# Fused attention and two MLP layers on one core: the second layer's weights converted first, layer one after all weights, blocks of one tile

## The chip, the cores and the metric

The kernel runs on one core of one Trainium2 chip. The metric is device time in microseconds (us), from the start to the end of one execution. Before the change it is 1220.09 us, the median of three runs (1217.87 to 1220.64).

## What is computed

The reference is, cut to what matters:

```python
# q, k, v: 4 batches x 8 heads x 576 rows x 64
scores = q @ k.T / 8
kth = 32nd largest of each row of scores
attn = softmax(where(scores >= kth, scores, -1e9))
x = (attn @ v), heads side by side            # 2304 x 512
h = x @ moe_w_in                              # 512 -> 2048
x = maximum(0.01 * h, h) @ moe_w_out          # 2048 -> 512
r = maximum(x @ moe2_w_in, 0)
out = (s * r * r + b) @ moe2_w_out
```

All tensors are float32, and the products are to keep that accuracy.

## The kernel before

Every float32 operand of a matmul is turned into two float16 halves ("hi" and "lo"), and each product is three float16 matmuls: hi x hi, hi x lo, lo x hi. The halves need a power-of-two scale found on the chip, so each of the four weight matrices ("1i", "1o" of layer one, "2i", "2o" of layer two, 16 units of 128 x 512 each) is converted first: `w_load` brings a unit (512 KB) from HBM, `w_rest`, `w_shift`, `w_sign` and `w_round` (ACT, DVE, ACT, POOL) round it to 24 bits, `w_norm` and `w_diag` measure a group of four units on PE and DVE, and `hi`, `lo_g`, `lo_d`, `lo_t` and their kin write the halves. What engine does the splitting is set for each unit by a letter of `WM`. The halves of 1i and 1o stay in SBUF (`wreg`, 32 units). Those of 2i and 2o don't fit: `w_out` stores them to a scratch in DRAM (`sc_2i`, `sc_2o`), and layer two streams them back for every block of rows (`load`, 512 KB for two units, through the four buffers of `wst`); one pair of loads, `kept_i` and `kept_o`, stays (`NRES`).

The 2304 rows are 18 tiles of 128. Attention works in units: one pair of heads of one tile, 72 units, four for a tile. Eight of them, of the two tiles that hold the last 64 rows of two batches each, take twice the matmuls. In a unit, per head: `qk` on PE, `s_ev` on ACT, then on DVE four `t_max` (the eight largest of each row) and three `t_rep` (take them out); the mask and the exponential go by way of DVE (`expo`, `mask`) or by way of POOL and ACT (`above`, `less`, `expo2`), as a letter of `MKE` and `MK` says; the result is split, turned by two DMA transposes (`e_turn`; in the first `EB` units on PE instead) and multiplied with v (`pv_mm`).

When all units of a block's tiles are done, the block goes through layer one and later layer two. `BLOCKS` says how many tiles a block has. `rows_in` scales and splits a tile's rows and turns them by a DMA transpose (`turn`). In `layer`, `m_in` multiplies one unit of the first weight (12 matmuls of 128 x T, T being 128 times the tiles of the block) into `h`, `a1` to `a5` apply the activation and split it (ACT and POOL), and `m_out` multiplies into `acc` (3 matmuls of 128 x 512 for a unit and a tile). A token `lane` lets one layer at a time run its `m_in`. Layer one's `a1` waits for `fin1`, the scales of 1i and 1o; layer two waits for `fin`, everything converted and stored.

The order of the work is set by a planner: `Plan.add` notes each step with its engine, an assumed duration, its dependences and a key, and `Plan.order` lets each engine take, whenever it is free, the ready step with the lowest key whose buffers are there. The result is a fixed order on every engine. All the numbers in the tables at the top (`W0`, `WD`, `KO`, `PAD`) are keys or allowances of this planner. Before the change, the keys place 1i and 1o first, 2o and 2i later among the attention units.

Of the kernel before, what the change touches and what calls it, by code (L numbers as in the profile page):

```python
# [13 lines left out]
I32 = mybir.dt.int32  # L14
# [51 lines left out]
PAD = {"e_turn": 0, "load": 0.65, "turn": 0, "PE": 0}  # L66
# [137 lines left out]
def kernel(  # L204
# [44 lines left out]
    PHASED = ("wst", "raw", "T", "nred", "cI", "hl")  # L249
# [4 lines left out]
              "wT": (flat_w, 512 * NU + 4096)}  # L254
# [106 lines left out]
    out_done, lo_done, scaled, rounded = {}, {}, {}, {}  # L361
    g_last, cs_last, gtok = None, None, None
    for m, f in order:
# [4 lines left out]
        def w_load(m=m, f=f):  # L368
            t = ring("wraw" if m == "1i" else "raw", [P, 1024], I32, f"raw_{m}_{f}")
            raw[m, f] = t  # L370
            w = wsrc[m].bitcast(I32)
            if m[1] == "i":
                nc.sync.dma_start(out=t.rearrange("p (c n) -> p c n", c=4),
                                  in_=w[:, 2 * P * f:2 * P * (f + 1)].rearrange("(c p) n -> p c n", p=P))
            else:
                nc.sync.dma_start(out=t, in_=w[P * f:P * (f + 1), :])

        def w_rest(m=m, f=f):

            wT[m, f] = ring("wT" if m == "1i" else "T", [P, 512], F32, f"T_{m}_{f}")  # L380
# [245 lines left out]
    for (b, p), U in sorted(first_unit.items(), key=lambda e: e[1]):  # L626
# [65 lines left out]
        def v_hi(b=b, p=p, i=i):  # L692
            vt = vhl[b, p] = vbufs[i % BUFS["vT"]]
            r = vn[b, p]
            nc.scalar.activation(r[:, 0:9, :], r[:, 0:9, :], AF.Copy, scale=cv[b, p])
            nc.scalar.copy(vt[:, 0, 0:512].rearrange("p (h r d) -> p h r d", h=2, r=4),
                           r.rearrange("p (h r) d -> p h r d", h=2)[:, :, 0:4, :])
            for h in range(2):
                a, c = slice(64 * h, 64 * h + 64), slice(512 + 64 * h, 576 + 64 * h)
                nc.scalar.copy(vt[a, 0, c], r[a, 4, :])  # L700

        def v_lo(b=b, p=p):
            vt, r = vhl[b, p], vn[b, p]
            nc.gpsimd.tensor_tensor(vt[:, 1, 0:512].rearrange("p (h r d) -> p h r d", h=2, r=4),
                                    r.rearrange("p (h r) d -> p h r d", h=2)[:, :, 0:4, :],
                                    vt[:, 0, 0:512].rearrange("p (h r d) -> p h r d", h=2, r=4), op=ALU.subtract)
            for h in range(2):
                a, c = slice(64 * h, 64 * h + 64), slice(512 + 64 * h, 576 + 64 * h)
                nc.gpsimd.tensor_tensor(vt[a, 1, c], r[a, 4, :], vt[a, 0, c], op=ALU.subtract)
# [18 lines left out]
    for u in range(NUN):  # L728
# [170 lines left out]
        for c, (j0, j1) in enumerate(((0, 4), (4, 8), (8, 9)) if u < EB else ()):  # L899
# [384 lines left out]
```

## Time and profile before

| | |
|---|---|
| median of three runs | 1220.09 us |
| the profiled execution, its time and its span | 1219.95 us, 1218.1 us |
| instructions in the span | 24846 |
| PE busy | 1054.8 us, 87% |
| DVE busy | 927.3 us, 76% |
| ACT busy | 888.8 us, 73% |
| POOL busy | 808.9 us, 66% |
| granted TensorE clock, mean | 0.94 |
| mean busy share of the 16 DMA engines (dynamic queue) | 66.3% |

PE is TensorE's matmuls, PEld its weight loads, DVE is VectorE, ACT ScalarE, POOL GpSimd, SP the engine that issues all DMAs. A matmul's busy time is modelled from a pipelined engine, so how fast PE goes is better read from the distance between the starts of two groups of a timeline. The granted clock is a share of full speed: 1.00 is 2.4 GHz, 0.50 would be 1.2 GHz.

### The profile page before, as it was taken

The numbers are of one execution on the slowest core, as the hardware profiler recorded it, in microseconds if no ns is written. First come the engines' busy times: TensorE is split into PE (matmuls) and PEld (weight loads), VectorE is DVE, ScalarE is ACT, GpSimd is POOL, SyncE is SP. The second block draws the span as 40 slices with busy tenths as digits, with TensorE's granted clock in tenths as the row PEclk, the third lists the DMA queues.
The fourth block names the chain that finished last, engine by engine and source line by source line (L and its number), as shares of the span: only waits on it lengthen the run. The fifth ranks groups of instructions, "written<-read, shape, count | busy, mean of one in ns | idle before, by whom it ended". The sixth has DMA issues, their size and how long they took to land.

```text
span 1218.1 us, 24846 instructions
## 1 busy us (share of the span) xinstructions
PE 1054.8 (87%) x8952; PEld 720.7 (59%) x8952; DVE 927.3 (76%) x2189; ACT 888.8 (73%) x1679; POOL 808.9 (66%) x1138
## 2 busy tenths in 40 slices
PE   2556665459979997999899999999999999999998
PEld 1324433236556755776666677676567776766665
DVE  3689899889995999998879999974996599710100
ACT  6999885587678777878888887876887486742432
POOL 6876444567667786868888787885886477832321
PEclk9676888679989998999999999999999999999999
DMA  8936355486878756984579986445797578662454
GB/s 260 295 56 186 121 182 188 131 203 150 210 131 217 188 105 118 233 164 85 106 147 223 245 210 147 76 93 139 178 225 202 99 155 214 128 175 78 137 190 141
DMA packets 349244, 198.84 MB, mean 163 GB/s; under 512 B 277696, under 2 KB 302272, under 8 KB 349120
## 3 DMA queue, kind: packets, MB, share of 16 engines
q1 hardware_dynamic: 349120, 197.25, 66.3%
q8 instruction: 70, 1.15, 0.4%
q14 instruction: 54, 0.44, 0.1%
HBM read 122.16 MB, written 13.11 MB: 111 GB/s over the span
## 4 chain that ended last, share of the span: by engine, by line
PE 37%; DVE 23%; ACT 15%; POOL 9%; DMA 8%; issue 5%; SPq 2%; DVEq 0%; ACTq 0%; POOLq 0%
PE h L1098 14%; PE acc L1168 14%; DVE mx L829 9%; DVE wk L838 8%; PE pv L973 3%; PE sc L811 2%; DMA a<-ehl 2%; POOL ehl L939 2%; ACT em L870 2%; POOL em L867 2%; POOL g L1146 1%; DMA raw_2i<-in_moe_w_in_dram 1%; ACT ehh L933 1%; DVE em L854 1%; DMA st_o<-sc_2o 1%
## 5 line engine op out<-in xcount | busy, mean ns | idle before, releaser
L829 DVE MAX8 mx<-wk 128x8 f32<-128x576 f32 x432 | 312.4, 746 | 0.7
L1168 PEld LDWEIGHTS <-g 128*128 128x128 f16 x1728 | 164.1, 99 | 141.0 <-issue 12.9
L1098 PE MATMUL h<-early,wreg 128*128 128x256 f16 (+1 forms) x1920 | 215.1, 263 | 0.5 <-ACT r L1127 0.5
L1168 PE MATMUL acc<-wreg,g 128*128 128x512 f16 x864 | 215.2, 379 | 0.0
L838 DVE MATCH_REPLACE8 wk<-mx,wk 128x576 f32<-128x576 f32 x288 | 212.7, 741 | 0.0
L1098 PEld LDWEIGHTS <-wreg 128*128 128x128 f16 x1920 | 174.8, 98 | 50.3 <-issue 1.1
L1168 PE MATMUL acc<-st_o,g 128*128 128x512 f16 x756 | 190.3, 379 | 1.7 <-DMA st_o<-sc_2o 1.7
L1098 PE MATMUL h<-xT,st_i 128*128 128x256 f16 (+1 forms) x1680 | 187.5, 262 | 0.4 <-ACT r L1130 0.2
L939 POOL TENSOR_TENSOR ehl<-em,ehh 128x576 f16<-128x576 f32 x130 | 167.3, 1293 | 16.4 <-DMA a<-ehl 7.5
L1098 PEld LDWEIGHTS <-st_i 128*128 128x128 f16 x1680 | 151.9, 98 | 42.4 <-DMA st_i<-sc_2i 1.4
L867 POOL TENSOR_TENSOR em<-s,em 128x576 f32<-128x576 f32 x96 | 136.0, 1431 | 19.2 <-ACT em L864 19.0
L1146 POOL TENSOR_TENSOR g<-early,g 128x512 f16<-128x512 f32 x72 | 83.4, 1159 | 72.2 <-ACT g L1143 71.8
L811 PE MATMUL sc<-kT,qT 128*128 128x288 f16 (+1 forms) x640 | 104.1, 303 | 29.9 <-ACT s L817 24.3
L1143 ACT ACTIVATE g<-r 128x512 f16<-128x512 f32 x144 | 89.7, 624 | 50.4 <-PE acc L1168 49.9
L1146 POOL TENSOR_TENSOR g<-r,g 128x512 f16<-128x512 f32 x72 | 84.7, 1177 | 62.1 <-ACT g L1143 60.1
L829 DVE MAX8 mx<-s 128x8 f32<-128x576 f32 x144 | 107.8, 749 | 12.6 <-ACT s L817 12.4
L817 ACT COPY s<-sc 128x576 f32<-128x576 f32 x144 | 91.2, 633 | 24.6 <-PE sc L811 24.1
L838 DVE MATCH_REPLACE8 wk<-mx,s 128x576 f32<-128x576 f32 x144 | 106.7, 741 | 0.0
L864 ACT ACTIVATE em<-s,st 128x576 f32<-128x576 f32 x96 | 71.1, 769 | 39.4 <-POOL st L858 35.4
L811 PEld LDWEIGHTS <-qT 128*128 128x128 f16 (+1 forms) x640 | 59.5, 106 | 63.4 <-issue 44.9
L933 ACT CAST ehh<-em 128x576 f16<-128x576 f32 x130 | 86.6, 667 | 13.4 <-DVE em L854 12.2
L870 ACT ACTIVATE em<-em,st,est 128x576 f32<-128x576 f32 x96 | 82.8, 863 | 15.0 <-POOL em L867 14.5
(209 smaller groups left out, 1745.5 us busy)
## 6 DMA issues: line engine op xcount, KB each, us to landing
st_i<-sc_2i SPq DMA_DIRECT2D x70, 512.0 KB, 4.3
st_o<-sc_2o SPq DMA_DIRECT2D x70, 512.0 KB, 4.3
raw_1o<-in_moe_w_out_dram SPq DMA_DIRECT2D x16, 512.0 KB, 4.2
wreg<-in_moe_w_in_dram SPq DMA_DIRECT2D x16, 512.0 KB, 6.3
raw_2o<-in_moe_w_out_dram SPq DMA_DIRECT2D x16, 512.0 KB, 3.4
raw_2i<-in_moe_w_in_dram SPq DMA_DIRECT2D x16, 512.0 KB, 4.4
qn<-in_q_dram SPq DMA_DIRECT2D x16, 256.0 KB, 4.2
sc_2o<-hl_2o SPq DMA_DIRECT2D x16, 256.0 KB, 2.7
```

Of the source, the lines that this page charges most:

```text
L811: nc.tensor.matmul(pt[a, c, 0:288], lhsT=qT[u][:, h, z, a], rhs=kT[b, p][:, 576 * h + 288 * c:576 * h + 288 * c + 288], start=(z == 0), st ...
L817: nc.scalar.copy(sc[u, h], box["pt"][:, :, 0:288])
L829: nc.vector.max(out=mx[u][:, h, r, :], in_=wk[u, h] if r else flat(sc[u, h]))
L838: nc.vector.match_replace(out=wk[u, h], in_to_replace=mx[u][:, h, r, :], in_values=src, imm_value=NEG)
L867: nc.gpsimd.tensor_tensor(em[u][:, h, :], flat(sc[u, h]), em[u][:, h, :], op=ALU.subtract)
L870: nc.scalar.activation(em[u][:, h, :], em[u][:, h, :], AF.Exp, bias=st[u][:, h:h + 1], scale=est[:, 0, u:u + 1], accum_out=st[u][:, 2 + h: ...
L933: nc.scalar.copy(ehl[u][0][:, 576 * h:576 * h + 576], em[u][:, h, :])
L939: nc.gpsimd.tensor_tensor(ehl[u][1][:, a], em[u][:, h, :], ehl[u][0][:, a], op=ALU.subtract)
L1098: nc.tensor.matmul(box["h"][:, n * T:(n + 1) * T], lhsT=w[:, ew, c, :], rhs=src[:, ex, c, :], start=(c == 0 and ew == 0 and ex == 0), stop ...
L1143: nc.scalar.activation(gt[:, 0], box["r1"], AF.Square if l else AF.Copy)
L1146: nc.gpsimd.tensor_tensor(ghl[i, l, g][:, 1], box["v"], ghl[i, l, g][:, 0], op=ALU.subtract)
L1168: nc.tensor.matmul(accs[i, l, tt], lhsT=ghl[i, l, g][:, eg, n * T + tt * P:n * T + (tt + 1) * P], rhs=w[:, ew], start=(f == 0 and eg == 0 ...
```

## The change

The order of the weights becomes 2o, 2i, 1i, 1o. Since `wreg` is empty until 1i and 1o are converted, its upper half (1o's place) serves 2o, 2i and 1i as landing and work buffers (`wraw`, four, and `wT`, eight), and eight units of its lower half serve as buffers for the halves of 2o and 2i on their way to DRAM (`hl`, eight in place of two). Units 8 to 15 of 1i therefore wait until units 8 to 15 of 2i have been stored. 1o lands in `raw` and `T` (eight in place of six). Layer one can start only when 1i and 1o, now the last, are done. The 18 tiles form 16 blocks of one tile and one of two, in place of eight blocks of two and two of one. The planner's keys, the splitting modes `WM`, the mask modes `MKE`, and `PAD` get other values; `SQ`, which names the engine of the squaring, is "A" in both. New options for keys and values (`KVM`, all "G") choose what was done before; one of `EBM`'s letters is "D", which moves three small subtractions of unit 2 from PE and ACT to DVE (`e_low`).

```diff
-... "raw": 2, "T": 6, "hl": 2, "wraw": 4, "wT": 8, "wst": 4,
+... "raw": 2, "T": 8, "hl": 8, "wraw": 4, "wT": 8, "wst": 4,
-WM = {"1i": "GAPP", "1o": "PPDP", "2o": "VPAV", "2i": "APPG"}
-ORDER = ("1i", "1o", "2o", "2i")
+WM = {"1i": "PDAA", "1o": "DAAG", "2o": "GPPV", "2i": "PPAV"}
+ORDER = ("2o", "2i", "1i", "1o")
-MKE = "DDDDDDDDADDADDADDAADAADA"
+MKE = "DADADADAAAAADADAAADADADA"
-EB = 7
+EB = 6
-W0 = {"1i": -32.95, "1o": -81.15, "2o": 9.16, "2i": -16.52}
-WD = {"1i": 0.038, "1o": 0.182, "2o": 0.322, "2i": 1.5}
+W0 = {"2o": -38.54, "2i": -51.71, "1i": -9.33, "1o": 3.35}
+WD = {"2o": 0.024, "2i": 0.068, "1i": 0.375, "1o": 0.199}
-KO = {"wl": -16.16, "wh": -41.37, "k": -33.06, "v": -8.31, "q": -56.3, "u0": 5.64, "u1": 11.13, "u2": -2.91, "kt": -33.14, "qh": -19.39}
+KO = {"wl": 15.86, "wh": 13.91, "k": -28.68, "v": -34.52, "q": -44.01, "u0": -4.83, "u1": 2.14, "u2": 32.26, "kt": -16.55, "qh": -21.94}
-BLOCKS = [2, 2, 2, 2, 2, 2, 1, 1, 2, 2]
+BLOCKS = [1, 1, 1, 1, 1, 1, 1, 1, 1, 1, 1, 1, 1, 1, 1, 1, 2]
-PAD = {"e_turn": 0, "load": 0.65, "turn": 0, "PE": 0}
+PAD = {"e_turn": 0, "load": 0, "turn": 4.29, "PE": 0}
...
-              "wT": (flat_w, 512 * NU + 4096)}
+              "wT": (flat_w, 512 * NU + 4096), "hl": (flat_w, 8 * 512)}
...
-            t = ring("wraw" if m == "1i" else "raw", [P, 1024], I32, f"raw_{m}_{f}")
+            t = ring("raw" if m == "1o" else "wraw", [P, 1024], I32, f"raw_{m}_{f}")
-            wT[m, f] = ring("wT" if m == "1i" else "T", [P, 512], F32, f"T_{m}_{f}")
+            wT[m, f] = ring("T" if m == "1o" else "wT", [P, 512], F32, f"T_{m}_{f}")
...
-            free = None if m != "1o" else lo_done["1i", ff] if ff >= 8 else rounded["1i", 12 + ff // 2]
+            if m == "1o":
+                free = [lo_done["1i", ff] if ff >= 8 else rounded["1i", 12 + ff // 2]]
+            else:
+                free = [x_ for x_ in (out_done[order[16 + ff]], cs_done.get(order[16 + ff]))] if m == "1i" and ff >= 8 else []
...

```

How it moves the order, at two places. First DVE, where the scales of layer one are finished. `w_shift` is L387 before, `t_max` and `t_rep` are L860 and L869 after, `lo_d` is L498 before, the last row of `fin1` is L585 before and L594 after. Before:

```order
L387 SCALAR_TENSOR_TENSOR T_2o_1264<-raw_2o_1190,T_2o_1264 128x512
L453 TENSOR_SCALAR cI_1o_1286<-ident,cg 128x128
L576 TENSOR_REDUCE consts<-cg 128x1
L325 TENSOR_SCALAR cg<-cg 128x4
L578 TENSOR_SCALAR cg<-cg,consts 128x4
L580 TENSOR_SCALAR consts<-consts 128x1
L576 TENSOR_REDUCE consts<-cg 128x1
L325 TENSOR_SCALAR cg<-cg 128x4
L578 TENSOR_SCALAR cg<-cg,consts 128x4
L580 TENSOR_SCALAR consts<-consts 128x1
L585 SCALAR_TENSOR_TENSOR cg<-cg 128x4
L498 SCALAR_TENSOR_TENSOR wreg<-T_1o_1117,cg,wreg 128x512
```

After:

```order
L860 MAX mx_2388<-s_1_2347 128x8
L860 MAX mx_2388<-wk_0_2392 128x8
L869 MATCH_REPLACE wk_1_2402<-mx_2388,s_1_2347 128x576
L585 TENSOR_REDUCE consts<-cg 128x1
L328 TENSOR_SCALAR cg<-cg 128x4
L587 TENSOR_SCALAR cg<-cg,consts 128x4
L589 TENSOR_SCALAR consts<-consts 128x1
L585 TENSOR_REDUCE consts<-cg 128x1
L328 TENSOR_SCALAR cg<-cg 128x4
L587 TENSOR_SCALAR cg<-cg,consts 128x4
L589 TENSOR_SCALAR consts<-consts 128x1
L594 SCALAR_TENSOR_TENSOR cg<-cg 128x4
```

Before, `fin1` stands at DVE's instruction 197, with 2o and 2i still to come; now it stands at 382, among the searches of unit 10 (`mx_2388` is that unit's buffer), with the rounding of all 64 units of weights ahead of it.

Second SP, where the first weights of layer two are fetched back. L943 and L980 are `e_turn` (the number behind `a_` is the attention unit), L1044 and L1081 `turn`, L781 and L812 `q_turn`, L1192 and L1229 the kept pair, L1077 and L1114 `load`. Before:

```order
L540 DMA sc_2i<-hl_2i_3042 128x1024
L1044 DMA_TRANSPOSE early<-xhl_2_3050 128x8x128
L943 DMA_TRANSPOSE a_13_3201<-ehh_3122 128x9x128
L781 DMA_TRANSPOSE qT_3218<-qhl_2965 128x8x128
L1192 DMA kept_i_3241<-sc_2i 128x2x1024
L1192 DMA kept_o_3247<-sc_2o 128x2x1024
L943 DMA_TRANSPOSE a_13_3261<-ehl_3162 128x9x128
L1077 DMA st_i_3271<-sc_2i 128x2x1024
L1077 DMA st_i_3276<-sc_2i 128x2x1024
L1077 DMA st_i_3284<-sc_2i 128x2x1024
L1077 DMA st_o_3291<-sc_2o 128x2x1024
L739 DMA qn_3298<-in_q_dram 128x8x64
```

After:

```order
L980 DMA_TRANSPOSE a_8_2386<-ehl_2372 128x9x128
L1081 DMA_TRANSPOSE early<-xhl_1_2296 128x8x128
L980 DMA_TRANSPOSE a_9_2555<-ehh_2513 128x9x128
L980 DMA_TRANSPOSE a_9_2584<-ehl_2535 128x9x128
L812 DMA_TRANSPOSE qT_2620<-qhl_2237 128x8x128
L1229 DMA kept_i_2660<-sc_2i 128x2x1024
L1229 DMA kept_o_2665<-sc_2o 128x2x1024
L1114 DMA st_i_2674<-sc_2i 128x2x1024
L1114 DMA st_i_2705<-sc_2i 128x2x1024
L1114 DMA st_i_2710<-sc_2i 128x2x1024
L1114 DMA st_i_2720<-sc_2i 128x2x1024
L770 DMA qn_2774<-in_q_dram 128x8x64
```

The kept pair and the first loads stood between the two transposes of unit 13 and right behind; they now stand ahead of those of unit 10, and behind them follow 238 loads in all, 14 for each of 17 blocks, where there were 140 for ten blocks.

## Rows read from the trace of the kernel before

**Rows 1.** The page, parts 1 and 2: engines, and the span in 40 slices.

```profile
span 1218.1 us, 24846 instructions
PE 1054.8 (87%) x8952; PEld 720.7 (59%) x8952; DVE 927.3 (76%) x2189; ACT 888.8 (73%) x1679; POOL 808.9 (66%) x1138
...
PE   2556665459979997999899999999999999999998
...
DVE  3689899889995999998879999974996599710100
...
PEclk9676888679989998999999999999999999999999
DMA  8936355486878756984579986445797578662454
```

**Rows 2.** Windows: stretch, length, busy us per engine, granted clock, DMA share, GB/s.

```profile
0.00:273.00 273.00, 150.69 (x862) 89.00 (x862) 220.38 (x517) 217.97 (x419) 167.08 (x230) 0.77 0.63 180
273.00:348.00 75.00, 64.51 (x543) 43.14 (x541) 73.02 (x178) 53.74 (x100) 53.48 (x70) 0.93 0.72 169
348.00:480.00 132.00, 120.81 (x1112) 86.28 (x1113) 111.96 (x277) 101.85 (x195) 96.04 (x153) 0.96 0.69 154
480.00:1080.00 600.00, 584.47 (x5538) 413.75 (x5536) 510.26 (x1198) 469.68 (x893) 457.88 (x659) 1.00 0.72 161
1080.00:1218.00 138.00, 134.32 (x907) 88.56 (x905) 11.64 (x23) 45.56 (x76) 34.44 (x30) 1.00 0.46 144
```

**Rows 3.** Timeline of PE where layer one starts: start, us, line, tiles, idle before.

```profile
271.99 1.57 PE L973 MATMUL pv<-vhl,a 128*128 128x128 f16 x25 [3.65 <-DMA a<-ehl]
273.37 3.99 PE L1098 MATMUL h<-early,wreg 128*128 128x256 f16 x24
```

**Rows 4.** Timeline of PE at two later waits.

```profile
347.94 4.25 PE L1098 MATMUL h<-xT,kept_i 128*128 128x256 f16 x24 [2.14 <-DMA xT<-xhl]
...
460.87 1.12 PE L811 MATMUL sc<-kT,qT 128*128 128x288 f16 x4 [5.77 <-ACT s L817]
```

**Rows 5.** Timeline of PE in a one-tile block, 936 to 939, and 1000 to 1009.

```profile
936.20 0.83 PE L1098 MATMUL h<-early,wreg 128*128 128x128 f16 x12
936.87 0.65 PE L811 MATMUL sc<-kT,qT 128*128 128x288 f16 x4
937.36 0.81 PE L1168 MATMUL acc<-st_o,g 128*128 128x512 f16 x3
938.01 0.83 PE L1098 MATMUL h<-early,wreg 128*128 128x128 f16 x12
...
1000.46 2.17 PE L1098 MATMUL h<-xT,st_i 128*128 128x128 f16 x36
1002.47 0.65 PE L811 MATMUL sc<-kT,qT 128*128 128x288 f16 x4
...
1004.36 1.47 PE L1098 MATMUL h<-early,wreg 128*128 128x256 f16 x12
1005.67 1.03 PE L973 MATMUL pv<-vhl,a 128*128 128x128 f16 x27
1006.53 1.47 PE L1098 MATMUL h<-early,wreg 128*128 128x256 f16 x12
```

**Rows 6.** The page, part 5: groups' count, busy us, mean ns.

```profile
L829 DVE MAX8 mx<-wk 128x8 f32<-128x576 f32 x432 | 312.4, 746 | 0.7
L838 DVE MATCH_REPLACE8 wk<-mx,wk 128x576 f32<-128x576 f32 x288 | 212.7, 741 | 0.0
L867 POOL TENSOR_TENSOR em<-s,em 128x576 f32<-128x576 f32 x96 | 136.0, 1431 | 19.2 <-ACT em L864 19.0
L1098 PEld LDWEIGHTS <-wreg 128*128 128x128 f16 x1920 | 174.8, 98 | 50.3 <-issue 1.1
```

**Rows 7.** Groups by line on DVE and POOL: the mask, rounding, splitting.

```profile
L854 DVE SCALAR_TENSOR_TENSOR em<-s,mx,em 128x576 f32<-128x576 f32 x48 | 45.7, 956 | 5.8 <-ACT em L851 5.5
L387 DVE SCALAR_TENSOR_TENSOR wreg<-wreg 128x512 int32<-128x512 int32 x16 | 16.1, 1016 | 9.1 <-ACT wreg L382 9.0
L387 DVE SCALAR_TENSOR_TENSOR T_2o<-raw_2o,T_2o 128x512 int32<-128x512 int32 x16 | 11.6, 722 | 1.2 <-ACT T_2o L382 1.2
```

**Rows 8.** Waits of SP's queue: line, releaser, us in total, times, longest.

```profile
SPq L376 <- POOL T_1o L397: 26.8, 8, 11.7
SPq L376 <- POOL T_2o L397: 26.5, 11, 8.0
```

**Rows 9.** DMA issues by line (count, KB, us to landing), and one window of 80 us.

```profile
st_i<-sc_2i SPq DMA_DIRECT2D x70, 512.0 KB, 4.3
st_o<-sc_2o SPq DMA_DIRECT2D x70, 512.0 KB, 4.3
...
640.00:720.00 80.00, 78.12 (x689) 54.93 (x689) 78.59 (x185) 68.25 (x131) 65.75 (x99) 1.00 0.96 228
```

**Rows 10.** Waits of PE for streamed weights, in all.

```profile
PE acc L1168 <- DMA st_o<-sc_2o: 1.7, 2, 1.1
```

More of the change, by code (lines that the diff above doesn't have):

```diff
@@ L420 @@
         x = add(ACT, REST, w_rest, [l], kk, take=[tT], use=[tr])
-        y = add(DVE, 0.62, w_shift, [x], kk, use=[tT, tr], lock=True)
+        y = add(DVE, 0.66, w_shift, [x], kk, use=[tT, tr], lock=True)
         x = add(ACT, SIGN, w_sign, [x], kk, use=[tr])
@@ L528 @@
                 x = add(PE, 0.86, lo_t, [i_], ks, take=[th] + out_tok, use=tI + [tT])
-                x = add(ACT, 0.478, hi_p, [x, free], ks, use=[th] + out_tok)
+                x = add(ACT, 0.478, hi_p, [x, *free], ks, use=[th] + out_tok)
                 if mode == "V":
@@ L669 @@
         ick_done[b, p] = add(DVE, 0.07, k_inv, [x], kk)
-        x = add(ACT, 0.667, k_scale, [x], kk, use=[tk])
-        x = add(ACT, 0.573, k_hi, [x], kk, use=[tk, th])
-        x = add(POOL, 1.234, k_lo, [x], kk, use=[tk, th])
+        if KVM[i] == "D":
+            x = add(ACT, 0.667, k_hi, [x], kk, use=[tk, th])
+            x = add(DVE, 0.75, k_low, [x], kk, use=[tk, th], lock=True)
+        else:
+            x = add(ACT, 0.667, k_scale, [x], kk, use=[tk])
+            x = add(ACT, 0.573, k_hi, [x], kk, use=[tk, th])
+            x = add(POOL, 1.234, k_lo, [x], kk, use=[tk, th])
         tok_kT[b, p] = token("kT")
@@ L698, in v_hi @@
             for h in range(2):
                 a, c = slice(64 * h, 64 * h + 64), slice(512 + 64 * h, 576 + 64 * h)
[L700 to L709, printed above, removed]
+                out.append((lambda e, a=a, c=c: vt[a, e, c], r[a, 4, :], a))
@@ L717 @@
         x = chain(DVE, pow2_steps(lambda b=b, p=p: cv[b, p], lambda box=box: box["pt"][:, 0:1], 1, 0.13), [x], key + KO["v"] + 0.2, use=[tt])
-        x = add(ACT, 1.63, v_hi, [x], key + KO["v"] + 0.2, use=[tv], take=[tV])
-        vT_done[b, p] = add(POOL, 1.65, v_lo, [x], key + KO["v"] + 0.2, use=[tv, tV])
+        x = add(ACT, 1.0 if KVM[i] == "D" else 1.63, v_hi, [x], key + KO["v"] + 0.2, use=[tv], take=[tV])
+        if KVM[i] == "D":
+            vT_done[b, p] = add(DVE, 1.0, v_lo, [x], key + KO["v"] + 0.2, use=[tv, tV], lock=True)
+        else:
+            vT_done[b, p] = add(POOL, 1.65, v_lo, [x], key + KO["v"] + 0.2, use=[tv, tV])
     qn, qhl, qT, icq_done, sc, wk, em, mx, st, ehl, ahl, pv, x32 = {}, {}, {}, {}, {}, {}, {}, {}, {}, {}, {}, {}, {}
@@ L926 @@
             x = add(ACT, 0.05 + 0.107 * n, e_hi2, [x, lo[0][0] if c else None], ke, use=[tt, *ta])
-            y = add(PE, 0.15 + 0.053 * n, e_sub, [x], ke, use=[tt, *ta])
-            lo.append((x, add(ACT, 0.05 + 0.107 * n, e_lo2, [y], ke, use=[tt, *ta])))
+            if EBM[u] == "D":
+                lo.append((x, add(DVE, 0.1 + 0.13 * n, e_low, [x], ke, use=[tt, *ta])))
+            else:
+                y = add(PE, 0.15 + 0.053 * n, e_sub, [x], ke, use=[tt, *ta])
+                lo.append((x, add(ACT, 0.05 + 0.107 * n, e_lo2, [y], ke, use=[tt, *ta])))
         def e_hi(u=u, h=0):
```

58 lines of the change are left out of this document (42 added, 16 removed).

## The prediction

> **What bounds the kernel now.** I read the engines and the slices first [rows 1]. PE is busy for 87% of the span, at 90% or more from the 17th slice on, while DVE is done at slice 35 of 40. The first quarter is different: PE is half idle and its granted clock mostly 0.6 to 0.9, DVE and ACT are busy. So there is a first stage in which PE waits for others, and a second in which PE is the bound. The windows put numbers on it [rows 2]: to 273 us PE has 151 us of work; from 480 to 1080 it is idle for 15.5 of 600 us, in the last 138 us for 3.7, which are the last output's way out. Layer one starts at 273.37 us [rows 3].
>
> So the time is: start of layer one, plus PE's work from there, plus what PE loses on the way. I price PE's work by distances between starts, not by busy times [rows 5]. Twelve matmuls of 128 x 256 take 1.31 us (1004.36 to 1005.67), twelve of 128 x 128 take 0.67 us (936.20 to 936.87), three of 128 x 512 take 0.65 us (937.36 to 938.01), four of `qk` 0.49 us (936.87 to 937.36), 27 of `pv_mm` 0.86 us (1005.67 to 1006.53). A tile in one layer has 16 units: 16 x (0.655 + 0.65) = 20.88 us in a block of two, 16 x (0.67 + 0.65) = 21.12 us alone. A unit of attention is 2 x 0.49 + 0.86 = 1.84 us, the eight double ones twice that.
>
> Before, from 273 us: 32 tile-layers in pairs and 4 alone are 752.7 us; attention has by PE's order 59 `qk` units and 62 `pv` units left, with the double ones 67 x 0.98 + 70 x 0.86 = 126 us; the rest of 2i is about 6 us (an estimate from its few matmuls). Sum 885 us. PE ends at about 1214 us, so 56 us are lost. Of these I find 21.7 us idle from 273 to 480 us, 9 us by the clock there (0.93 and 0.96), 15.5 us idle later [rows 2]; some 10 us remain in small gaps.
>
> **The change, part by part.** All sums are made against the profiled execution: span 1218.1 us, 1.85 us more around it, 1219.95 us, which is the median of the runs within 0.1 us.
>
> *Order of the weights.* No step is added; all 64 units are converted ahead of layer one rather than 60 or so. What counts is the work that stands ahead of it on each engine, and attention gets less: nine `pv` units done at layer one's start in place of ten. On DVE, up to the scales of layer one, against DVE's work up to 273 us before: 4 searches and 3 replacements fewer (7 x 0.75 = 5 us less), 10 masks fewer (9.6 us less), 6 roundings more (4.3 to 6.1 us more), some 5 us more of small splits [rows 6, 7]. Sum: about 4 us less. ACT comes out about 4 us longer by the same count. POOL has 11 more splits, 3 more roundings and 10 more of `less`, about 26 us, on top of the 167 it was busy for in 273 us. POOL is the least loaded of the three in that stretch, DVE and ACT stand idle for some 55 us each [rows 2], so I cost POOL's part at nothing; if it lay wholly on the path it would be 26 us. Against it, loads of weights waited 53 us in all for their two landing buffers [rows 8], and now have four. Some of the idle time should close. I take layer one's start at 272 us; the ends are 258 (a quarter of the idle time closes) and 299 (POOL's 26 us in full).
>
> *Blocks of one tile.* Seven blocks of two are split: 7 x 2 layers x 16 units x (2 x 0.67 - 1.31 = 0.03 us) = 6.7 us more on PE. The weight loads double with the small matmuls, and one takes 98 ns on PEld [rows 6], longer than the 56 ns between two such matmuls, but rows of 36 in sequence still run at 2.01/36 = 56 ns [rows 5], so they hide. Here a rule speaks against the change: the Trainium skill ("TensorE: Matmul & The Clock Gate", section "Back-to-back issue gap") gives about 81 ns for each matmul in a sustained stream with 128 columns. By that the split would cost (81 - 56) ns for each of 5376 new matmuls, an estimate of 134 us; this trace has 56 ns, so I keep 6.7 us.
>
> PE's work from 272 us is then 32 x 21.12 + 4 x 20.88 = 759.4 us, less 2.7 us for 48 matmuls that PE does early; attention has 60.5 `qk` and 63 `pv` units left, 128 us; no weights. Sum 885 us, the same as before.
>
> *What PE loses early.* Before, 31 us to 480 us. The waits there are layer two's first matmuls waiting for the block's turned rows, and PE held in order behind a `qk` whose score buffer is not free [rows 4]. Layer one has a pair of tiles then, and the next pair needs eight more units of attention. With single tiles, two whole tiles are ready when layer one starts, and each next one needs four units. By PE's order, 15 `pv` units (double ones counted twice) stand ahead of 42 us of layer work before and of about 68 us after; at 31 units it is 160 and 198 us. I take 10 us.
>
> *Loads of layer two.* 17 blocks x 14 loads are 238 in place of 140. In the last window the DMA engines move 144 GB/s at a share of 0.46, 313 GB/s when busy, so 512 KB take 1.67 us; 98 more take 164 us of all 16 engines. From 273 us on the engines are busy for 0.72 x 75 + 0.69 x 132 + 0.72 x 600 + 0.46 x 138 = 641 us [rows 2]; it becomes 805 us. By PE's order 125 us of layer work remain behind the last `pv_mm` (141 before); it takes some 40 loads, 67 us. So 738 us of transfers fall between 272 us and the end of attention, where PE has 760 us of work and perhaps 805 us to do it in: a share of 0.92. Before, it was about 0.72, with 0.96 for one stretch of 80 us, in which PE still lost only 1.9 us [rows 9]. Waits for streamed weights were 1.7 us [rows 10]. That cover, transfers with room to spare, is what the change uses up. I add one wait of about 0.6 us for each block, 10 us, to the late loss of 23.
>
> SP issues 98 more DMAs, and a `load` that waits for its `wst` buffer holds the `e_turn` and `turn` behind it, which release `pv_mm` and `m_in`; I cost that within the same 10 us, since attention is ahead: DVE's searches end over 100 us before PE does.
>
> Sum: 272 + 885 + 10 + 33 = 1200, plus 3.8 to the end of the span and 1.85 around it: **1206 us**, 14 less than before.
>
> **The rivals.**
> *The DMA engines become the bound (slower).* For: a share of 0.92 for 800 us, four buffers, 4.3 us from issue to landing [rows 9], one queue in order. Against: 0.96 was sustained for 80 us. The end of attention is then 272 + 738/share, and 125 + 6 us follow. At 0.90 it is 1223 us; that is the point from which it decides. At 0.87 it is 1251 us.
> *The start moves further.* If a quarter of the idle time closes: 258 + 885 + 38 + 6 = 1187 us. For: waits for buffers [rows 8]. Against: POOL's 26 us.
> *Nothing is gained.* What the early stage wins is lost later: 273 + 885 + 56 + 6 = 1220 us. So too if the single blocks only shift the waits that single pairs had.
> *Small matmuls wait for their weight loads.* 98 ns each rather than 56: 5376 x 42 ns = 226 us more, 1430 us. Only the rule above speaks for it, and by its own figure it would be less; rows 5 speak against.
>
> **How the numbers follow.** Forecast 0.42, start earlier 0.12, nothing gained 0.12, DMA bound 0.32, small matmuls 0.02. A measurement of this kernel tells 0.2%, 2.4 us, from no change. Of "nothing gained" I put 0.08 within that and 0.02 on each side, so: faster 0.56, same 0.08, slower 0.36. The forecast's own range is 1195 to 1217 us, from the start's ends and the late loss. The range over the cases goes from 1182 (an early start with somewhat fewer losses) to 1252 (DMA at 0.87).
>
> **What would show it.** Right: layer one's twelves come at 0.67 us distance and start near 272 us; from there PE is idle for under 45 us; the DMA share is about 0.9 to the end of attention; the tail behind the last `pv_mm` is near 125 us. Wrong: waits of PE or PEld for `st_i` and `st_o` of tens of us, or `pv_mm` waiting for `a` again and again (DMA bound); a start after 290 us (POOL on the path); twelves at 1 us (weight loads).

## The result and the profile after

The changed kernel takes **1208.3 us**, the median of six runs (1204.23 to 1211.08); the kernel before takes 1220.37 us beside it (six runs). The ratio is 0.9903, with a 95% interval of 0.9884 to 0.9923: faster by about 12 us. The forecast was 1206 us, 14 us less than before. The profiled execution took 1208.34 us, 1206.6 us of it the span.

The page, parts 1 and 2, answers to [rows 1]:

```profile
span 1206.6 us, 30307 instructions
PE 1044.3 (87%) x11589; PEld 754.8 (63%) x11589; DVE 918.5 (76%) x2164; ACT 892.5 (74%) x1696; POOL 844.5 (70%) x1169
...
PE   1675666239999999999999989999999999999988
...
PEclk9876677658999999999999999999999999999999
DMA  8987872347799999989999998999898998974274
```

PE's row jumps from 3 to 9 at the 10th slice and stays there but for a few 8s, where it dipped to 7 twice before. The price is in the last row: the DMA engines, mostly at 4 to 8 before, are at 9 in 20 of the 40 slices. The windows, with the columns of [rows 2]:

```profile
0.00:273.00 273.00, 143.50 (x884) 90.29 (x885) 222.25 (x491) 222.66 (x430) 203.77 (x250) 0.73 0.68 195
273.00:348.00 75.00, 73.35 (x925) 56.25 (x923) 73.04 (x180) 57.98 (x111) 55.17 (x78) 0.97 0.83 171
348.00:480.00 132.00, 127.97 (x1603) 94.72 (x1603) 101.78 (x256) 101.53 (x196) 95.62 (x149) 1.00 1.00 234
480.00:1080.00 600.00, 583.39 (x7311) 436.58 (x7307) 516.37 (x1222) 470.49 (x897) 461.24 (x669) 1.00 0.96 224
1080.00:1207.00 127.00, 116.07 (x876) 76.94 (x876) 5.11 (x19) 39.84 (x66) 28.73 (x25) 0.98 0.49 156
```

From 273 to 480 us PE is idle for 1.7 + 4.0 = 5.7 us, where it was idle for 21.7; from 480 to 1080 us for 16.6 (15.5 before); behind that for 10.9 of 127 us (3.7 before). The timeline of PE, with the columns of [rows 3], at the start of layer one, at the longest later wait, at the last `pv_mm` and in the tail. (Four units of layer one's `m_in`, 48 matmuls, run ahead of it, from 194.44 us on; what follows them has to wait for the scales of 1i and 1o.)

```profile
272.19 4.00 PE L1135 MATMUL h<-early,wreg 128*128 128x128 f16 x36 [2.76 <-ACT r L1164]
...
278.33 0.83 PE L1135 MATMUL h<-early,wreg 128*128 128x128 f16 x12
279.00 0.81 PE L1205 MATMUL acc<-wreg,g 128*128 128x512 f16 x3
...
713.73 2.00 PE L1135 MATMUL h<-xT,st_i 128*128 128x128 f16 x24 [4.14 <-DMA st_i<-sc_2i]
...
1067.62 1.03 PE L1010 MATMUL pv<-vhl,a 128*128 128x128 f16 x27
...
1150.04 1.46 PE L1205 MATMUL acc<-st_o,g 128*128 128x512 f16 x6 [2.08 <-DMA st_o<-sc_2o]
1153.95 1.41 PE L1205 MATMUL acc<-st_o,g 128*128 128x512 f16 x5 [2.46 <-DMA st_o<-sc_2o]
...
1195.81 6.85 PE L1205 MATMUL acc<-st_o,g 128*128 128x512 f16 x31
```

PE's waits for transfers in the whole span (us, times, longest):

```profile
PE acc L1205 <- DMA st_o<-sc_2o: 11.8, 12, 2.5
PE pv L1010 <- DMA a<-ehl: 10.8, 7, 4.3
PE h L1135 <- DMA st_i<-sc_2i: 9.0, 9, 4.1
```

The first and third make 20.8 us of waits for streamed weights, some 19 more than before [rows 10]. In exchange, other waits between 480 and 1080 us are gone. This is that stretch in the kernel before, for the score buffer and for the scaled rows:

```profile
PE sc L811 <- ACT s L817: 6.1, 7, 2.4
PE acc L1168 <- ACT xs L1020: 4.3, 4, 2.1
```

In the changed kernel the first is 0.8 us there, and the second no longer appears. The DMA issues, answering to [rows 9], take 0.6 to 0.8 us longer to land:

```profile
st_i<-sc_2i SPq DMA_DIRECT2D x119, 512.0 KB, 4.9
st_o<-sc_2o SPq DMA_DIRECT2D x119, 512.0 KB, 5.1
```

### The profile page after: what moved, and what is told of

Same layout as the page of the kernel before. It is cut to its first block, busy times and chain, and to the rows that moved or that the text cites. A ratio compares the mean times of both kernels' runs of the same rounds, so it can differ in the third digit from the quotient of the medians.

```text
span 1206.6 us, 30307 instructions
## 1 busy us (share of the span) xinstructions
PE 1044.3 (87%) x11589; PEld 754.8 (63%) x11589; DVE 918.5 (76%) x2164; ACT 892.5 (74%) x1696; POOL 844.5 (70%) x1169
## 4 chain that ended last, share of the span: by engine, by line
PE 43%; DVE 17%; DMA 12%; ACT 11%; POOL 11%; issue 4%; SPq 2%; DVEq 0%; POOLq 0%; ACTq 0%
PE h L1135 17%; PE acc L1205 17%; DVE mx L860 7%; DVE wk L869 6%; DMA st_o<-sc_2o 4%; PE pv L1010 3%; PE sc L842 3%; POOL ehl L976 2%; DMA a<-ehl 2%; POOL g L1183 2%; DMA st_i<-sc_2i 2%; POOL em L898 2%; ACT wreg L386 1%; ACT wreg L397 1%; ACT em L901 1%
## 5 line engine op out<-in xcount | busy, mean ns | idle before, releaser
L860 DVE MAX8 mx<-wk 128x8 f32<-128x576 f32 x432 | 313.2, 747 | 0.9
L1135 PEld LDWEIGHTS <-wreg 128*128 128x128 f16 x3264 | 211.0, 99 | 54.0 <-issue 6.4
L1135 PE MATMUL h<-early,wreg 128*128 128x128 f16 (+1 forms) x3264 | 235.1, 224 | 2.8 <-ACT r L1164 2.8
L1205 PE MATMUL acc<-wreg,g 128*128 128x512 f16 x864 | 231.3, 379 | 0.0
L869 DVE MATCH_REPLACE8 wk<-mx,wk 128x576 f32<-128x576 f32 x288 | 212.8, 741 | 0.0
L1205 PE MATMUL acc<-st_o,g 128*128 128x512 f16 x756 | 200.6, 382 | 12.5 <-DMA st_o<-sc_2o 11.8
L1135 PEld LDWEIGHTS <-st_i 128*128 128x128 f16 x2856 | 179.7, 98 | 48.9 <-DMA st_i<-sc_2i 12.5
L1135 PE MATMUL h<-xT,st_i 128*128 128x128 f16 (+1 forms) x2856 | 201.4, 223 | 9.1 <-DMA st_i<-sc_2i 9.0
L898 POOL TENSOR_TENSOR em<-s,em 128x576 f32<-128x576 f32 x110 | 155.9, 1432 | 22.9 <-ACT em L895 22.7
L860 DVE MAX8 mx<-s 128x8 f32<-128x576 f32 x144 | 107.9, 750 | 23.0 <-ACT s L848 22.7
L895 ACT ACTIVATE em<-s,st 128x576 f32<-128x576 f32 x110 | 82.2, 768 | 41.9 <-POOL st L889 37.5
L901 ACT ACTIVATE em<-em,st,est 128x576 f32<-128x576 f32 x110 | 94.7, 862 | 17.1 <-POOL em L898 16.8
L869 DVE MATCH_REPLACE8 wk<-mx,s 128x576 f32<-128x576 f32 x144 | 106.8, 742 | 0.0
L1180 ACT ACTIVATE g<-r 128x512 f16<-128x512 f32 x144 | 89.5, 622 | 18.5 <-PE acc L1205 17.8
L1167 ACT ACTIVATE r<-h,cg 128x512 f32<-128x512 f32 x72 | 49.1, 682 | 67.0 <-PE h L1135 65.9
```

The lines of the kernel that those rows point to most:

```text
L860: nc.vector.max(out=mx[u][:, h, r, :], in_=wk[u, h] if r else flat(sc[u, h]))
L869: nc.vector.match_replace(out=wk[u, h], in_to_replace=mx[u][:, h, r, :], in_values=src, imm_value=NEG)
L895: nc.scalar.activation(em[u][:, h, :], flat(sc[u, h]), AF.Relu, bias=st[u][:, 8 + h:9 + h], scale=-BIG)
L898: nc.gpsimd.tensor_tensor(em[u][:, h, :], flat(sc[u, h]), em[u][:, h, :], op=ALU.subtract)
L901: nc.scalar.activation(em[u][:, h, :], em[u][:, h, :], AF.Exp, bias=st[u][:, h:h + 1], scale=est[:, 0, u:u + 1], accum_out=st[u][:, 2 + h: ...
L1135: nc.tensor.matmul(box["h"][:, n * T:(n + 1) * T], lhsT=w[:, ew, c, :], rhs=src[:, ex, c, :], start=(c == 0 and ew == 0 and ex == 0), stop ...
```

## The experiments

The question is which part of the change holds the 12 us: the order of the weights, the blocks of one tile, or the numbers that the planner got with them; and what the loads cost. Ratios are against the kernel before, run beside each set.

**1. The order of the weights alone.** In the changed kernel:

```diff
-BLOCKS = [1, 1, 1, 1, 1, 1, 1, 1, 1, 1, 1, 1, 1, 1, 1, 1, 2]
+BLOCKS = [2, 2, 2, 2, 2, 2, 1, 1, 2, 2]
```

> The changed kernel with the blocks of before (eight of two tiles, two of one) and all else of the change: the order of the weights alone. The planner plans anew. Theory (the blocks of one tile won the early stage and paid for it in loads): PE is idle again for 18 to 25 us between the start of layer one and 480 us (5.7 us in the changed kernel), the waits for st_i and st_o fall from 20.8 us to under 4, the twelves of 128 columns become 256 (6.7 us less), the tail's waits for st_o go; sum 1208 + 23 - 18 - 6.7 + about 5 for waits of pairs on their rows = 1212, between 1207 and 1220. Rival A (the order of the weights won the early stage, the single blocks only cost): the early idle time stays under 10 us and 20 to 25 us of waits and small matmuls go, 1183 to 1192. Rival B (order and blocks are worth something only together): 1220 or more, with layer one starting later than 280 us because a pair needs eight units.

Measured: 1249.6 us, ratio 1.0251 (1.0234 to 1.0267), slower than either kernel. Windows and timeline of PE:

```profile
273.00:348.00 75.00, 56.81 (x473) 39.64 (x473) 69.59 (x178) 48.42 (x93) 48.20 (x66) 0.89 0.58 122
348.00:480.00 132.00, 120.78 (x1107) 83.80 (x1105) 106.14 (x255) 101.89 (x196) 96.12 (x156) 0.94 0.69 152
480.00:1080.00 600.00, 562.49 (x5258) 396.35 (x5255) 518.36 (x1215) 461.42 (x875) 455.12 (x661) 0.98 0.69 157
```

```profile
326.33 1.12 PE L842 MATMUL sc<-kT,qT 128*128 128x288 f16 x4 [4.51 <-ACT s L848]
...
337.80 1.18 PE L842 MATMUL sc<-kT,qT 128*64 128x288 f16 x8 [6.02 <-ACT s L848]
```

The early idle time came back, as the theory had it, and more of it (18.2 + 11.2 = 29.4 us up to 480, where the theory said 18 to 25). But 37.5 us of idle time between 480 and 1080 us came too, and no theory had that. The start is at 274.74 us, so that rival B's reason, a later start, isn't it. Three times, at 321, 446 and 569 us, PE has no layer matmul for 15 to 21 us: a pair is through and the next one isn't ready.

**2. The blocks alone.** In the kernel before:

```diff
-BLOCKS = [2, 2, 2, 2, 2, 2, 1, 1, 2, 2]
+BLOCKS = [1, 1, 1, 1, 1, 1, 1, 1, 1, 1, 1, 1, 1, 1, 1, 1, 2]
```

> The kernel before with sixteen blocks of one tile and one of two, and nothing else of the change: the blocks alone, in the old order of the weights. Theory: the early idle time falls from 21.7 us to about 8, 98 loads more bring waits of some 20 us for st_i and st_o, small matmuls 6.7 us: between 1203 and 1215, about 1208, and the start of layer one near 273 us. Rival A (the order of the weights is what counts): early idle time over 18 us, and the loads' cost on top, 1230 to 1245. Rival B (only both together): layer one starts earlier than 265 us, since one tile needs four units, but layer two's first weights come later than one tile's layer one, so that PE waits over 20 us for them before 400 us; 1215 to 1230.

Measured: 1237.73 us, ratio 1.0167 (1.0139 to 1.0194).

```profile
273.00:348.00 75.00, 59.62 (x720) 43.70 (x719) 73.86 (x185) 53.88 (x98) 48.81 (x80) 0.95 0.83 205
348.00:480.00 132.00, 121.89 (x1516) 89.94 (x1516) 102.23 (x253) 96.53 (x186) 91.58 (x142) 0.99 0.92 219
```

PE is idle for 25.5 us from 273 to 480 us. The number is rival A's, but the first experiment spoke against rival A. The start is rival B's: layer one begins at 157 us and does one tile by 198 us. Then it has no matmul for 72 us, until the second tile's turned rows are there (rival B had PE wait for layer two's weights):

```profile
270.26 1.44 PE L1098 MATMUL h<-early,wreg 128*128 128x128 f16 x12 [1.18 <-DMA early<-xhl]
```

Each part alone loses, so either both belong together, or the planner's keys, which the change sets anew, fit one combination each. Experiments 5 to 8 tell these apart.

**3. Half the bytes of each load**, the order on every engine unchanged:

```diff
-nc.sync.dma_start(out=w.rearrange("p u e n -> p u (e n)"),
-                  in_=sc16["2" + kind][2 * j:2 * j + 2].rearrange("u p n -> p u n"))
+nc.sync.dma_start(out=w[:, 0].rearrange("p e n -> p (e n)"), in_=sc16["2" + kind][2 * j])
...
-return w[:, f % 2]
+return w[:, f % 2] if (io, f // 2) in kept else w[:, 0]
```

> The changed kernel with the same order on every engine, but each load of layer two brings only the first of its two units (256 KB in place of 512 KB) and the second unit's matmuls use the first one's weights: the streamed units with odd numbers are left out of the result. Only the bytes are halved. Theory (the DMA engines' share sets the waits for streamed weights): 238 x 0.84 us = 199 us of transfers less, share from 348 to 1080 us near 0.7, waits of PE for st_i and st_o from 20.8 us to under 5, waits of pv for the turned rows from 10.8 us to under 5: 1208 - 16 - 6 = 1186, between 1182 and 1193. Rival (the waits come of the order on SP's queue and of buffers that come free late, not of bytes): the waits stay over 12 us, 1200 to 1208.

Measured: 1191.13 us, ratio 0.9762 (0.9741 to 0.9784); the changed kernel has 0.9903. The theory holds: bytes alone, with the queue's order the same, are worth some 17 us. In one point it missed. The waits of `pv_mm` for turned rows stay, 10.3 us after 10.8, and most of them lie ahead of layer one (7.7 and 7.0 us), where no load of layer two runs yet. The window from 480 to 1080 us, then the waits for streamed weights, the first line from that window and the second from behind it:

```profile
480.00:1080.00 600.00, 587.49 (x7402) 441.93 (x7400) 518.23 (x1227) 474.20 (x905) 464.63 (x674) 1.00 0.73 158
```

```profile
PE h L1134 <- DMA st_i<-sc_2i: 0.7, 2, 0.5
...
PE acc L1204 <- DMA st_o<-sc_2o: 1.5, 2, 0.9
```

**4. Four single blocks, then pairs.** In the changed kernel:

```diff
-BLOCKS = [1, 1, 1, 1, 1, 1, 1, 1, 1, 1, 1, 1, 1, 1, 1, 1, 2]
+BLOCKS = [1, 1, 1, 1, 2, 2, 2, 2, 2, 2, 2]
```

> The changed kernel with four blocks of one tile first, then seven of two: 154 loads in place of 238, the planner plans anew. Theory (single blocks are worth something only while layer one and two get going): idle time up to 480 us stays under 10 us, waits for st_i and st_o fall under 5 us, small matmuls give back 5.6 us: 1208 - 15 - 5.6 = 1188, between 1183 and 1198. Rival (pairs have their own waits wherever they stand, for the second tile's units and for rows between the layers): what the loads give back is lost at the pairs, 1203 to 1215, with waits of m_in for turned rows of over 10 us.

Measured: 1243.57 us, ratio 1.0189 (1.0165 to 1.0212). Both missed. Up to 480 us PE is idle for 11.6 us (5.7 in the changed kernel); then the pairs begin, and it is idle for another 43.3 us by 1080. It runs dry (has no layer matmul) for 19 us at 562 us, where the first pairs take over:

```profile
480.00:1080.00 600.00, 556.69 (x4966) 390.84 (x4964) 517.18 (x1216) 461.30 (x878) 455.95 (x668) 0.97 0.68 156
```

**5 to 8. All four combinations, with keys fitted to each.** The same search, equally long for each, varied `W0`, `WD`, `KO`, `PAD`, `MKE`, `EB` and `WM` on the planner's own assumed durations; nothing else differs from experiments 1 and 2 and from the two kernels. The edit that makes the eighth out of the changed kernel (in the other three `WM` changes too):

```diff
-MKE = "DADADADAAAAADADAAADADADA"
+MKE = "DDAAADADDADAADDDDDAADDDA"
-EB = 6
+EB = 9
-W0 = {"2o": -38.54, "2i": -51.71, "1i": -9.33, "1o": 3.35}
+W0 = {"2o": -39.34, "2i": -41.29, "1i": -7.1, "1o": 4.15}
-WD = {"2o": 0.024, "2i": 0.068, "1i": 0.375, "1o": 0.199}
+WD = {"2o": 0.159, "2i": 1.55, "1i": 0.172, "1o": 0.151}
-KO = {"wl": 15.86, "wh": 13.91, "k": -28.68, "v": -34.52, "q": -44.01, "u0": -4.83, "u1": 2.14, "u2": 32.26, "kt": -16.55, "qh": -21.94}
+KO = {"wl": 17.81, "wh": 5.86, "k": -26.91, "v": -16.99, "q": -49.9, "u0": -6.27, "u1": -0.6, "u2": 55.77, "kt": -6.92, "qh": -32.92}
-PAD = {"e_turn": 0, "load": 0, "turn": 4.29, "PE": 0}
+PAD = {"e_turn": 0, "load": 0, "turn": 0.1, "PE": 0}
```

Five, six, seven and eight in turn:

> The first experiment again (new order of the weights, blocks of before), with the planner's keys, its allowances and the modes WM, MKE and EB searched anew for this combination, on the planner's own assumed durations; the same search, equally long, stands behind this run and the three beside it. Theory K (the keys of the change belong to its single blocks, and the first experiment lost its time by plans that leave PE without layer work): no stretch of over 12 us without layer matmuls from layer one on, idle time from 273 to 1080 us from 66.9 us to under 35 us, 1195 to 1215. Rival P (a pair needs eight units and the weights are ready only at 272 us, so that pairs run dry with any keys): 1235 or more, with qk waits of over 15 us between 273 and 480 us.

> The second experiment again (old order of the weights, blocks of one tile), with keys, allowances and modes searched anew for it in the same way. Theory K: the order of the weights matters little once the keys fit, 1195 to 1212, idle time from layer one to 480 us under 12 us, waits for st_i and st_o of 15 to 25 us as in the changed kernel. Rival O (in the old order 2o and 2i are still converted beside layer one and hold PE, ACT and SP): 1220 or more, with idle time of over 20 us up to 480 us.

> The kernel before with nothing changed but its keys, allowances and modes, searched anew in the same way. Theory K: its 21.7 us of early idle time and 9 us of clock are a matter of the plan, and half of it can be had without the change, 1200 to 1212, so that the keys alone are worth about as much as the change. Rival (blocks and order are what the change lives on): 1215 to 1230, early idle time of 18 us or more.

> The changed kernel with its keys, allowances and modes searched anew in the same way. Theory K: the plan starts layer one after fewer units, and its start moves some 5 to 10 us earlier, while the DMA share of 0.96 to 1.00 and the 20 us of waits for streamed weights stay: 1196 to 1206. Rival (transfers bound the middle already, an earlier start only moves the waits): 1206 to 1215 with waits for st_i and st_o of over 28 us.

Measured, with the idle time of PE from 273 to 1080 us by the windows:

| | blocks of before | blocks of one |
|---|---|---|
| old order, keys of its kernel | 1220.37; 37.2 us idle | (2) 1237.73, 1.0167; 50.8 us |
| new order, keys of its kernel | (1) 1249.6, 1.0251; 66.9 us | 1208.3, 0.9903; 22.3 us |
| old order, fitted | (7) 1197.67, 0.9836 (0.9818 to 0.9854); 40.3 us | (6) 1192.19, 0.9797 (0.9767 to 0.9826); 25.4 us |
| new order, fitted | (5) 1202.34, 0.9876 (0.9859 to 0.9893); 44.3 us | (8) 1184.05, 0.9730 (0.9712 to 0.9748); 22.9 us |

Three things follow, where "keys" stands for keys, allowances and modes; which of them did it was not separated. First, keys count for more than the change: the kernel before gains 1.6% by them alone, and experiments 1 and 2 lost their time by ill-fitting keys. Second, with keys fitted on both sides the change is still worth 1.1% (0.9730 against 0.9836), as much as it brought as it stood. Third, the parts depend on each other. The order alone is 0.4% slower with pairs (5 against 7). The single blocks alone may be 0.4% faster in the old order, but the intervals of 6 and 7 overlap, so that is unclear. Together they win.

What the four runs expected came only in part. The fifth has theory K's time, and no stretch without layer matmuls is over 10.5 us, but its idle time is 44.3 us and not under 35. The sixth and the seventh are faster than theory K said, and not for its reason. From layer one's start to 480 us PE is idle for 35.0 us in the sixth (from 165.92 us on), which was its rival's sign, and for 29.1 us in the seventh (from 206.74 us on), where theory K had the early idle time halve. What the seventh has instead is a start 67 us earlier than before the change.

So the table's idle time, which begins at 273 us, leaves out part of the loss in the old order. From layer one's start to 1080 us it is 41.6 us in the seventh and 50.8 us in the sixth, against 44.3 us in the fifth and 22.9 us in the eighth. Single blocks halve it in the new order; in the old one they don't.

What the order does is seen where layer one starts. The seventh kernel (old order, pairs, fitted) in windows:

```profile
207.00:276.00 69.00, 67.65 (x553) 44.86 (x552) 65.58 (x146) 59.16 (x110) 59.60 (x68) 0.99 0.82 210
276.00:325.00 49.00, 29.48 (x186) 15.98 (x185) 45.47 (x112) 40.78 (x76) 38.10 (x51) 0.75 0.86 208
```

It starts layer one at 206.74 us, as the old order allows, does the first pair, and then has no layer matmul for 48 us while 2o and 2i are still converted; the clock falls as well. The sixth (old order, single blocks) does the layer one of one tile from 165.92 us to 204 us, and its next layer matmul comes 70 us later, again when the second tile's turned rows are there:

```profile
274.42 0.83 PE L1098 MATMUL h<-early,wreg 128*128 128x128 f16 x12 [0.16 <-DMA early<-xhl]
```

The fifth (new order, pairs) starts at 253.09 us and runs dry four times for 8 to 11 us, behind its first pairs. The eighth starts a little earlier and from there never runs dry for over 6 us. Its start, and its window from 480 to 1080 us:

```profile
250.34 2.93 PE L1135 MATMUL h<-early,wreg 128*128 128x128 f16 x26 [2.27 <-ACT r L1164]
```

```profile
480.00:1080.00 600.00, 582.95 (x7193) 436.59 (x7191) 495.77 (x1183) 462.14 (x878) 451.89 (x651) 0.99 0.95 224
```

Theory K expected its start 5 to 10 us earlier; it is 22 us, where the whole gain over the changed kernel is 24 us. Its waits for streamed weights fell as well, from 20.8 to 10.5 us, where theory K had them stay. So both theories of that run were too low on what the keys could give. One reservation: the search goes by assumed durations and was made once for each combination. How far another search would move a time was not measured, so differences of 0.4% between fitted kernels, and to a lesser degree the 1.1%, may be the search's as much as the combination's.

**9. More work on POOL before layer one**, the order unchanged, in `w_round`:

```diff
+r = raw[m, f].rearrange("p (n t) -> p n t", t=2)[:, 0:P, 0]
+nc.gpsimd.tensor_tensor(r, r, r, op=ALU.add)
```

> The changed kernel with the same order on every engine, and one more small operation of POOL behind each of the 64 roundings (128 x 128, written over words that nobody reads any more): some 0.4 us each, about 26 us in all, as much as I had costed at nothing on POOL. Theory (POOL has room before layer one): layer one starts at 272 to 277 us and the time is 1207 to 1214. Rival (POOL's part lies on the path to layer one): the start moves by 15 to 26 us, 1222 to 1235.

Measured: 1213.26 us, ratio 0.9972 (0.9956 to 0.9989). The groups of POOL up to 273 us and the timeline:

```profile
L403 POOL TENSOR_TENSOR wreg<-wreg 128x128 int32<-128x128 int32 x48 | 28.1, 585 | 3.8
...
L403 POOL TENSOR_TENSOR raw_1o<-raw_1o 128x128 int32<-128x128 int32 x16 | 9.0, 560 | 1.3
```

```profile
277.49 2.72 PE L1137 MATMUL h<-early,wreg 128*128 128x128 f16 x24 [2.02 <-ACT r L1166]
```

The operation took 0.58 us rather than 0.4, so 37 us were added. The start moved by 5.3 us, half a microsecond past the theory's range, and the time by 5 (8 by the ratios), within it: POOL hides about six parts in seven, not all.

**10. Layer two for two tiles at a time**, layer one in single tiles, keys fitted anew. In the eighth kernel, with layer one's last block split too, and `LATE` a new key:

```diff
+PAIRS = [2, 2, 2, 2, 2, 2, 2, 2, 2]
...
-nt = len(blocks[i])
+nt = len(blks[l][i])
...
-base = 2.0 * sum(len(b) for b in blocks[:i]) + (1.0 if l else 0.0)
+base = 2.0 * blks[l][i][-1] + 1.0 + LATE if l else 2.0 * blks[l][i][0]
...
-            acc = layer(i, 0, tX, ready, tY[i])
+            acc = layer(i, 0, tX, ready, tY[i2] if i == mine[0] else None)
```

> The eighth kernel (changed kernel, fitted keys) with layer one still in single tiles, now all 18, but layer two for two tiles at a time: nine passes over the streamed weights, 126 loads in place of 238; keys fitted anew by the same search. Theory (a single tile is worth having where layer one starts and feeds PE, and costs only where layer two streams its weights): DMA share of 480 to 1080 us from 0.95 to under 0.75, waits for st_i and st_o from some 10 us to under 4, small matmuls of layer two gone (4 us less): 1164 to 1178. Rival (pairs in layer two run dry as pairs did in the first experiment, or an m_out for two tiles holds both acc buffers, which layer one then waits for): 1184 or more.

Measured: 1177.52 us, ratio 0.9668 (0.9640 to 0.9695), the fastest whole kernel here, 3.3% under the kernel before. Window and waits from 480 to 1080 us:

```profile
480.00:1080.00 600.00, 584.71 (x6366) 424.93 (x6364) 510.51 (x1203) 463.60 (x885) 458.35 (x659) 1.00 0.66 148
```

```profile
PE sc L844 <- ACT s L850: 8.8, 8, 3.3
PE pv L1012 <- DMA a<-ehl: 2.2, 3, 1.1
PE acc L1210 <- DMA st_o<-sc_2o: 1.7, 1, 1.7
```

The transfers are out of the way, yet only some 7 us came of it, and that can't be put to the pairs alone, since with this plan layer one also goes on 14 us earlier than in the eighth:

```profile
236.53 4.34 PE L1140 MATMUL h<-early,wreg 128*128 128x128 f16 x48 [2.08 <-ACT r L1169]
```

Part of what the transfers give back is lost to other waits, for the score buffer above all (8.8 us from 480 to 1080 us, 2.7 in the eighth), and up to 480 us PE is idle for 19.8 us (5.9 in the eighth). What layer two in pairs is worth by itself isn't shown.

**11. Half the bytes in the eighth kernel**, by the edit of the third.

> The eighth kernel (changed kernel, fitted keys) with the same order on every engine and half the bytes of each load, as in the third experiment (the streamed units with odd numbers are left out of the result). Theory (the fitted plan has fewer waits for streamed weights, some 10.9 us with those of pv for turned rows at 7.7, so less to win than the 17 us of the third): 1172 to 1179. Rival (PE is now waiting for other things and the transfers are hidden): 1181 to 1185.

Measured: 1161.65 us, ratio 0.9550 (0.9526 to 0.9575), 22 us under the eighth kernel and more than the theory gave:

```profile
480.00:1080.00 600.00, 591.16 (x7278) 443.03 (x7275) 493.87 (x1178) 462.24 (x880) 452.39 (x651) 1.00 0.71 154
```

PE's idle time there falls from 17.1 to 8.8 us and its clock from 0.99 goes back to 1.00. By the profiled executions the span is 18.5 us shorter: 12 us of that are idle time, 6 us are PE's busy time. The waits for streamed weights fell by only 7.8 us, from 10.5 to 2.7, so they are not all that the bytes cost. Whether the bytes count for more here (22 us) than in the changed kernel (17 us), the intervals leave open.

## Why the prediction was right, step by step

- **Start of layer one**: forecast 272 us, measured 272.19. POOL's part, costed at nothing, was larger than its 26 us: up to 273 us POOL was busy for 203.8 us after 167.1, 36.7 us more. It was mostly hidden all the same. Experiment 9 puts the price of such work at 5.3/37, by which 36.7 us would be some 5 us (an estimate). The landing buffers did less than hoped: loads of weights still waited 64.9 us for one, 26.0 of it for 1o, which lands in the two of `raw` as before; it was 74.4 us before (the 53 of [rows 8], and 21.1 for units of 2i and 1i). That the sum of such parts came out at nothing is in part luck. The range down to 258 us was too cautious: fitted keys move the start to 250 us with the same amount of conversion.
- **PE's work from there**: twelve matmuls of 128 columns come at 0.67 us (278.33 to 279.00), as taken from [rows 5]. The Trainium skill ("TensorE: Matmul & The Clock Gate", section "Back-to-back issue gap") has about 81 ns for each in a sustained stream. This trace has 56 ns in a kernel with 6144 of them, and the 134 us that the rule would have added didn't come.
- **Early loss**: forecast 10 us, measured 5.7 us idle and, by the clock of 0.97 in 73 us of work, about 2 us. The reason given, that a single tile is ready sooner and leaves no hole behind it, is shown for the new order by experiments 5 and 8: from layer one's start to 480 us PE is idle for 17.6 us with pairs and 5.9 with single blocks. In the old order it doesn't hold (29.1 and 35.0 us, experiments 7 and 6). That the blocks do it by themselves, which the prediction let one believe, is not so: experiments 1, 2 and 4 lost 29 to 41 us against the changed kernel. Fitted keys gave that back to the first two; the fourth was not fitted.
- **Late loss**: forecast 33 us. Of these 23 were carried over from before, and by the prediction's own sums (56 lost, 31 of them early) it should have been 25. Measured: 16.6 us idle from 480 us, 10.9 - 3.8 = 7.1 us behind 1080, some 2 us of clock there (0.98); and what is left, 1206.6 - 272.2 - 885 - 7.9 - 26 - 3.8 = 11.7 us, is no idle time by the windows. It lies where PE counts as busy, and no row that I read shows it. Together about 37 us. Within it two terms were off and nearly cancelled. The 98 loads cost 19 us of waits and not 10; some 14 of them are late, and 4.5 are most of the early idle time. And 10 us of other late waits, which I had carried over from before, went away. Single blocks also end these: in the fitted kernels the waits for the score buffer from 480 to 1080 us are 2.2 and 2.7 us with single blocks, 5.4 and 6.7 us with pairs.
- **DMA**: forecast a share of 0.92; measured 1.00 for 132 us and 0.96 for 600. By the windows the engines are busy for 62 + 132 + 576 + 62 = 832 us from 273 us on, 191 more than before and not 164. Put to the 98 loads alone that is 1.95 us for each and not 1.67 (and rather more, since before the change some transfers of 2i's conversion came after 273 us, the last store at 313 us). That the transfers didn't become the bound was right, but not by the arithmetic of that rival, which took 0.90 for a ceiling: it was passed for over 700 us.
- **Tail**: forecast 125 us of layer work behind the last `pv_mm`. It stands at 1067.62, 0.86 us long, and PE ends at 1195.81 + 6.85 = 1202.7: 134 us: the 125, some 7 us of idle time, two waits of which are shown above, and 2 us of clock.

In sum the forecast was 2 us off the median. The mechanism was right: the early loss went, and the loads took back part of it. The 19 us of waits against 10 is the term that was mis-sized. That it was offset by waits that I left standing was luck, and so the 2 us flatter the forecast.

## What to carry to other kernels

Where one engine is the bound and others feed it, look for the stretches in which it has none of the big, movable work: smaller blocks close them, and the price is the data that every block fetches again. Judge a change of blocks or of order only with a plan fitted to it: here single blocks in the old order were 1.7% slower than pairs with the keys of the kernel before, and no slower (0.4% faster, within the intervals) with keys fitted to each. And try the block size by stage where stages pay differently: single tiles in the stage with resident weights, pairs in the one that streams them, was the fastest version, though its start was earlier too.

## What the runs showed of the hardware

- A share of the DMA engines is not a price for bytes. In the tail, where almost only the loads run, they moved 156 GB/s at a share of 0.49, 318 GB/s when busy; from 480 to 1080 us, beside the transposes of attention, 224 GB/s at 0.96, which is 233. A cost taken from the quiet stretch, as I took it, comes out too low (an estimate of 1.67 us for 512 KB, where the windows gave 1.95).
- A share of 1.00 is not a limit, and it can cost little. From 348 to 480 us, at 1.00, PE was idle for 4.0 of 132 us, and for 40 us the share even read 1.11 in the changed kernel, so it isn't a plain fraction of the time:

```profile
600.00:640.00 40.00, 38.77 (x463) 28.59 (x461) 33.41 (x87) 35.00 (x70) 32.55 (x56) 1.00 1.11 263
```

- Fewer bytes also speed up what shares the queue. With half loads (experiment 3) the transposes of attention landed in 3.4 us in place of 4.8 and 4.4:

```profile
a<-ehh SPq DMA_TRANSPOSE x66, 3.4
a<-ehl SPq DMA_TRANSPOSE x66, 3.4
```

- On POOL a fourth of the columns is not a fourth of the time: 128 x 128 took 585 ns where 128 x 512 took 1381 (int32, experiment 9, mean of 48 each; the smaller one works on every other word).
